# Another order of TensorE's work where one batch's MLP ends and the next one's begins

## The chip, the cores and the metric

The kernel runs on one core of a Trainium2 chip. The metric is device time in microseconds (us) of one execution. Three runs of the kernel before gave 1241.06, 1241.08 and 1241.23 us, so the median is 1241.08 us. All profile numbers come from one further, profiled execution that took 1240.99 us.

## What is computed

The reference is linear attention followed by a token mixer and a two-layer MLP, all in float32 accuracy, for 8 batches of 576 tokens and 512 features (8 heads of 64):

```python
def phi(x):
    proj = np.einsum('bhsd,df->bhsf', x, w_phi)
    proj = proj - np.max(np.abs(proj), axis=-1, keepdims=True)
    return np.concatenate([np.exp(proj), np.exp(-proj)], axis=-1)
q_p, k_p = (phi(q), phi(k))
kv = np.einsum('bhsf,bhsd->bhfd', k_p, v)
z = np.sum(k_p, axis=2)
num = np.einsum('bhsf,bhfd->bhsd', q_p, kv)
den = np.einsum('bhsf,bhf->bhs', q_p, z)[..., None] + 1e-06
x = num / den                       # heads side by side: (batch, 576, 512)
h = x.transpose(0, 2, 1) @ U @ V    # U: 576 x 32, V: 32 x 576
u = x + h.transpose(0, 2, 1)
out = u + np.maximum(u @ w_ch1, 0.0) @ w_ch2   # 512 -> 2048 -> 512
```

## The kernel before

**Two streams of work share TensorE.** The first is the attention of a batch: four pairs of heads, each cut into steps. `s_k0` projects k's 64 tail tokens (tile `pkt`) and the first head (`pk`), `s_k1` the second head, `s_q0` and `s_q1` project q (`pqt`, `pq`), `s_kv` makes k-features times v (`kv_ps`), `s_out` multiplies with the q-features (`xp`) and writes the result into `x` and, for the tail tokens, `xt`. `transpose_k` and `transpose_q` bring the raw k and q of the pair after the next one into shape (tiles `tT`, `T`). The second stream is the MLP of the batch before. Float32 accuracy is made of split values (`_hi`, `_lo`), so each product takes three matmuls.

**The MLP of a group of 512 tokens** (`Mixer`, line 564) begins with four `transposes(t)` (571): four TensorE transposes of `x[:, t, :]` into a PSUM tile `pt`, then ScalarE copies it to `uT_hi` and VectorE subtracts to get `uT_lo` (`split_t`, 223: lines 224 and 225). Then come 32 chunks from `chunks()` (635): `hidden(f)` (582, tile `ph`, twelve 512-column matmuls at line 588, then ScalarE's `h_hi` at 593 and VectorE's `h_lo` at 594) and `add(f)` (598, twelve matmuls at 605 into the four tiles `o`), in the order h0, h1, a0, h2, a1, ..., h15, a14, a15. Below, h15 stands for `hidden(15)`, a15 for `add(15)`, and h0', h1', a0' for those of the next group. `add(13)` also issues four loads of the token mixer's result from DRAM (`st`, line 612), and a15 ends in `finish()` (617): four VectorE additions of `o` to `st` (622) and the stores. There are nine groups: one for each batch, and one for the tail tokens of all batches, `x_tail`.

**The token mixer** (`Tokens`, 508) works on `x` in the last pair of a batch: `split`, `down`, then `up(0)` to `up(3)` and `up(NT)` for the tail tokens (549): one matmul (tile `vp`, 559), one VectorE addition into `x` or `xt` (560), one store.

**What limits the order.** PSUM has eight banks (line 67): three of tag `at` for all short-lived tiles (`pkt`, `pk`, `pq`, `xp`, `vp`, `T`, `pt`), one of tag `ph` for the hidden layer, and four of tag `o`. For groups 0 and 1, `pt` of tiles 2 and 3 uses `o` banks (line 572), and for the last two groups every second `ph` uses an `at` bank (583). `uT_hi` and `uT_lo` have one buffer each: no part of the new group's may be written before the old group's h15 has read the old one. `x` and `xt` have one buffer each too.

**Who sets the order.** In the first two batches a planner arranges all engines. From the third batch on, `ordered` (736) writes TensorE's order by hand (`manual_schedule`, line 860): `mix()` (655) takes the next chunk from the list `todo`. The other engines and the DMA queues are still ordered by the planner, from its own estimate of times, and then execute their queues in order. Within a batch `ordered` puts one chunk between any two attention steps. At a batch's end it runs `mix(len(todo) - HELD)` with HELD = 4, which leaves a13, h15, a14, a15, and then

```python
m.transposes(0)
tk.up(NT)
mix()               # a13
m.transposes(1)
m.transposes(2)
mix()               # h15
m.transposes(3)
do(far, "transpose_q")
todo.extend(m.chunks())
```

The next pair's turn then goes on with `s_k0`, a14, `s_out`, a15, `s_k1`, h0', `s_q0`, h1'. After the last batch, `x_tail` is loaded and its four transposes are laid between a13, h15, a14 and a15 (797 to 805).

Of the kernel before, what the change touches and what calls it, by code (L numbers as in the profile page):

```python
# [25 lines left out]
def tile_kernel(  # L26
# [13 lines left out]
    B, H, S, D = q.shape  # L40
# [7 lines left out]
    NT = S // P  # L48
# [41 lines left out]
    def load_w_phi():  # L90

        for g in range(2):
            nc.sync.dma_start(out=w_f[g * D:(g + 1) * D, :], in_=w_phi)
        nc.gpsimd.memset(w_two, 0.0)
        for g in range(2):
            r_ = slice(g * D, (g + 1) * D)
            nc.vector.tensor_copy(out=w_two[r_, g, :], in_=w_f[r_, :])
        nc.vector.tensor_copy(out=w_hi, in_=w_f)
        nc.vector.tensor_sub(w_lo, w_f, f32(w_hi))
# [62 lines left out]
    def load_uv():  # L162
        st = stage("u_st")[:, 0:(NT + 1) * R, :]
        sv = st.rearrange("p (t r) w -> p t r w", r=R)
        nc.sync.dma_start(
            out=sv[:, 0:NT], in_=U[0:SM].rearrange("(p t) r w -> p t r w", t=NT))
        for g in range(2):
            nc.sync.dma_start(out=sv[g * ST:(g + 1) * ST, NT], in_=U[SM:S])
        u_f = convert(st, "u").rearrange("p (t r) -> p t r", r=R)
        nc.vector.memset(f32(u_all[:, NT:NT + 2]), 0.0)  # L170
        parts = [(slice(0, P), slice(0, NT), slice(0, NT))]
        for g in range(2):
            parts.append((slice(g * ST, (g + 1) * ST), slice(NT + g, NT + g + 1), slice(NT, NT + 1)))
        for pr, to, of in parts:
            nc.vector.tensor_copy(out=u_all[pr, to, 0, :], in_=u_f[pr, of])
            nc.vector.tensor_sub(u_all[pr, to, 1, :], u_f[pr, of], f32(u_all[pr, to, 0, :]))
            for i in (2, 3):
                nc.vector.tensor_copy(out=u_all[pr, to, i, :], in_=f32(u_all[pr, to, 0, :]))

        for cs in (slice(0, SM // 2), slice(SM // 2, SM), slice(SM, S)):  # L180
            n = cs.stop - cs.start
            st = stage(f"v_st{cs.start}")[:, 0:n, :]
            for g in range(4):
                nc.sync.dma_start(out=st[g * R:(g + 1) * R], in_=V[:, cs])
            v_f = convert(st, f"v{cs.start}")
            vm = v_all[:, cs]
            if cs.stop <= SM:
                ps_ = slice(cs.start // NT, cs.stop // NT)
                v_f = v_f.rearrange("r (p t) -> r t p", t=NT)
                vm = v_all[:, 0:SM].rearrange("r (t p) -> r t p", t=NT)[:, :, ps_]  # L190
            nc.vector.tensor_copy(out=vm, in_=v_f)
            lo = slice(3 * R, 4 * R)
            nc.vector.tensor_sub(vm[lo], v_f[lo], f32(vm[lo]))
# [453 lines left out]
    def weights(upto):  # L647

        while done_f[0] < upto:
            f = next(blocks, None)  # L650
            done_f[0] = NFC if f is None else f - 1

    todo = []

    def mix(n=1):
        for _ in range(n):
            if todo:
                fn, f = todo.pop(0)
                if fn.__self__.g == 0 and done_f[0] < NFC:
                    weights(f + 2)  # L660
                fn(f)
# [22 lines left out]
    def keep_busy(n, here=False):  # L684
        wp = ps("busy", "ph")
        for _ in range(n):
            ins = nc.tensor.matmul(wp, zeros[:, 0:P], zeros, start=True, stop=True)
            if here:
                tc.keep_in_program_order(ins)

    HELD = 4
# [41 lines left out]

    ORDERED = 2

    def ordered(cur, nxt, x, xt, tk):

        for n, (b, j) in list(enumerate(pairs))[ORDERED * NPAIR:]:
            last = j == NPAIR - 1
            far = Pair(*pairs[n + 2]) if n + 2 < len(pairs) else None  # L740

            def do(who, name):
                if who is not None:
                    getattr(who, name)()

            if far is not None:
                far.load_v()
            do(nxt, "s_k0")
            mix()
            cur.s_out(x, xt)  # L750
            if j == 1:
                tk.split(0)
            if last:
                tk.split(1)
            mix()
            do(nxt, "s_k1")
            mix()
            do(nxt, "s_q0")
            mix()
            if last:  # L760
                tk.down(1)
            do(nxt, "s_kv")
            do(far, "transpose_k")
            mix()
            if last:
                tk.up(0)
                tk.up(1)
                mix()
                tk.up(2)
                tk.up(3)  # L770
            do(nxt, "s_q1")
            if j == 1:
                tk.down(0)
            if not last:
                mix()
                do(far, "transpose_q")
                mix()
            else:
                mix(len(todo) - HELD)
                m = Mixer(b, x)  # L780
                m.transposes(0)
                tk.up(NT)
                mix()
                m.transposes(1)
                m.transposes(2)
                mix()
                m.transposes(3)
                do(far, "transpose_q")
                todo.extend(m.chunks())
                if nxt is not None:  # L790
                    if b % 2 == 1:
                        xt = moe.tile([P, C], F32, tag="xt", name=f"xt{b + 1}")
                        nc.vector.memset(xt[ST:P], 0.0)
                    x = moe.tile([P, NT, C], F32, tag="x", name=f"x{b + 1}")
                    tk = Tokens(b + 1, x, xt)
            cur, nxt = nxt, far
        mix(len(todo) - HELD)
        x = moe.tile([P, NT, C], F32, tag="x", name="x_tail")
        nc.sync.dma_start(out=x, in_=u_dram[B])
        m = Mixer(B, x)  # L800
        for t in range(NT):
            m.transposes(t)
            mix()
        todo.extend(m.chunks())
        mix(len(todo))

    if True:
        cur = Pair(0, 0)
        load_w_phi()
        cur.load_v()  # L810
        keep_busy(6)
        cur.transposes()
        cur.s_k0()
        cur.s_k1_qt()
        cur.s_q0_only()
        nxt = Pair(0, 1)
        nxt.load_v()
        nxt.transposes()
        load_uv()
        cur.s_kv0_q1()  # L820
        cur.s_kv1()
        x = moe.tile([P, NT, C], F32, tag="x", name="x0")
        xt = moe.tile([P, C], F32, tag="xt", name="xt0")
        nc.vector.memset(xt[ST:P], 0.0)
        tk = Tokens(0, x, xt)
        for n, (b, j) in enumerate(pairs[:ORDERED * NPAIR]):

            far = Pair(*pairs[n + 2]) if n + 2 < len(pairs) else None
            if far is not None:
                far.load_v()  # L830
            if nxt is not None:
                step(nxt.s_k0)
            step(cur.s_out0, x, xt)
            if nxt is not None:
                step(nxt.s_k1_qt)
            step(cur.s_out1, x)
            if j == 1:
                tk.split(0)
            if j == NPAIR - 1:
                fill = []  # L840
                if nxt is not None:
                    fill = [nxt.s_q0_only, far.transposes, nxt.s_kv0_q1, nxt.s_kv1]
                tokens(tk, fill)
                if nxt is not None:
                    pace = Pace(32 - HELD, 34)
                    if b % 2 == 1:
                        xt = moe.tile([P, C], F32, tag="xt", name=f"xt{b + 1}")
                        nc.vector.memset(xt[ST:P], 0.0)
                    x = moe.tile([P, NT, C], F32, tag="x", name=f"x{b + 1}")
                    tk = Tokens(b + 1, x, xt)  # L850
            else:
                step(nxt.s_q0_only)
                if j == 1:
                    step(tk.down, 0)
                if far is not None:
                    step(far.transposes)
                step(nxt.s_kv0_q1)
                step(nxt.s_kv1)
            cur, nxt = nxt, far
        with tc.manual_schedule(engines={nc.tensor.engine}):  # L860
            ordered(cur, nxt, x, xt, tk)


# [29 lines left out]
```

## Time and profile before

| what | value |
|---|---|
| median of three runs | 1241.08 us |
| profiled execution: time, and span from the first to the last instruction | 1240.99 us, 1239.1 us |
| TensorE matmuls busy | 1177.0 us (95%) |
| TensorE weight loads busy | 957.5 us (77%) |
| VectorE, ScalarE, GpSimd busy | 679.5 us (55%), 545.7 us (44%), 205.4 us (17%) |
| granted TensorE clock, mean over the span | 0.985 |
| chain that ended last | TensorE 78%, VectorE 17%, ScalarE 2% |

The hand-ordered part begins near 250 us and ends at the span's end. In the views, a row of the timeline gives the start, the duration, the engine, the line, and in brackets the idle time of the engine ahead of it with the instruction that ended it. PE is TensorE, PEld its weight loads, DVE is VectorE, ACT is ScalarE, SPq the DMA-issuing queue of SyncE. Because matmuls are pipelined, their rows overlap: one 512-column matmul lasts 0.39 us in its row, and the next starts 0.23 us after it. The distance between starts is what counts.

### The profile page before, as it was taken

What the parts mean: (1) busy time and instruction counts of PE and PEld (TensorE: products, weight loads), DVE (VectorE), ACT (ScalarE), POOL (GpSimd) and SP (SyncE); (2) the same over time, 40 slices, a digit from 0 to 9 for tenths busy, and PEclk for the clock granted to TensorE, in tenths of its full rate; (3) what the DMA queues carried; (4) which work ended last, traced back from release to release, by engine and by line L of the source; (5) the groups of instructions that cost most, each with busy time, mean ns of one, the idle gap of its engine ahead of it and who ended that gap; (6) DMA issues with size and microseconds to landing.
All of it is one profiled execution on the core that took longest, in us unless ns stands there. A gap on an engine that the chain in (4) does not pass through costs nothing.

```text
span 1239.1 us, 22887 instructions
## 1 busy us (share of the span) xinstructions
PE 1177.0 (95%) x9266; PEld 957.5 (77%) x9280; DVE 679.5 (55%) x1469; ACT 545.7 (44%) x1230; POOL 205.4 (17%) x184
## 2 busy tenths in 40 slices
PE   8998888789999999999998999999999999999998
PEld 5666666568887888778887888778877887888886
DVE  6569989966464655456545646565545643212111
ACT  6667777745443445345434544354434531011110
POOL 3235444311110111011110111012101110000000
PEclk9999999999998999999999999899999999999999
DMA  4244344321131112221121113111222002100101
GB/s 132 53 143 126 101 142 138 113 99 43 30 92 41 42 30 61 71 63 30 56 68 54 40 30 96 41 38 30 61 70 64 27 1 83 66 1 1 34 1 34
DMA packets 95176, 75.70 MB, mean 61 GB/s; under 512 B 52320, under 2 KB 77280, under 8 KB 94944
## 3 DMA queue, kind: packets, MB, share of 16 engines
q1 hardware_dynamic: 95072, 74.25, 20.1%
q8 instruction: 73, 1.20, 0.4%
q14 instruction: 31, 0.25, 0.1%
HBM read 55.35 MB, written 18.87 MB: 60 GB/s over the span
## 4 chain that ended last, share of the span: by engine, by line
PE 78%; DVE 17%; ACT 2%; issue 1%; DMA 1%; SPq 0%; POOL 0%; DVEq 0%; POOLq 0%; ACTq 0%
PE o L605 28%; PE ph L588 28%; PE kv_ps L412 4%; PE xp L437 4%; DVE w L142 2%; PE pk L369 2%; PE T L298 2%; DVE w_ab L150 2%; PE pp L543 1%; PE kv_ps L403 1%; DVE uT_lo L225 1%; DVE h_lo L594 1%; DVE w_ab L147 1%; DVE w_lo L219 1%; DVE st L622 1%
## 5 line engine op out<-in xcount | busy, mean ns | idle before, releaser
L594 DVE SCALAR_TENSOR_TENSOR h_lo<-ph,h_hi 128x512 fp32r<-128x512 f32 x144 | 99.3, 689 | 285.9 <-ACT h_hi L593 285.6
L588 PE MATMUL ph<-uT_hi,w_hi 128*128 128x512 f32 x576 | 231.9, 403 | 10.0 <-DVE h_lo L594 8.2
L605 PE MATMUL o<-w_hi,h_hi 128*128 128x512 f32 x576 | 234.6, 407 | 5.0 <-ACT h_hi L593 5.0
L605 PE MATMUL o<-w_lo,h_hi 128*128 128x512 f32 x576 | 228.5, 397 | 0.0
L588 PE MATMUL ph<-uT_lo,w_hi 128*128 128x512 f32 x576 | 226.6, 393 | 1.3 <-DVE uT_lo L225 1.3
L588 PE MATMUL ph<-uT_hi,w_lo 128*128 128x512 f32 x576 | 227.1, 394 | 0.0
L605 PE MATMUL o<-w_hi,h_lo 128*128 128x512 f32 x576 | 225.4, 397 | 0.0
L593 ACT ACTIVATE h_hi<-ph 128x512 fp32r<-128x512 f32 x144 | 85.7, 595 | 275.8 <-PE ph L588 275.7
L333 POOL PARTITION_ALL_REDUCE qp<-qp x64 | 127.6, 1994 | 229.9 <-ACT qp L332 227.3
L588 PEld LDWEIGHTS ph<-uT_hi,w_hi 128*128 128x128 f32 x576 | 109.1, 189 | 35.2 <-DVE h_lo L594 11.7
L605 PEld LDWEIGHTS o<-w_hi,h_hi 128*128 128x128 f32 x576 | 110.5, 192 | 29.0 <-ACT h_hi L593 6.5
L605 PEld LDWEIGHTS o<-w_hi,h_lo 128*128 128x128 f32 x576 | 110.4, 192 | 25.1 <-issue 0.7
L588 PEld LDWEIGHTS ph<-uT_hi,w_lo 128*128 128x128 f32 x576 | 109.1, 189 | 24.0
L588 PEld LDWEIGHTS ph<-uT_lo,w_hi 128*128 128x128 f32 x576 | 109.5, 190 | 22.7 <-DVE uT_lo L225 1.6
L605 PEld LDWEIGHTS o<-w_lo,h_hi 128*128 128x128 f32 x576 | 110.5, 192 | 20.9
L333 POOL PARTITION_ALL_REDUCE qp_t<-qp_t x32 | 24.4, 763 | 472.0 <-ACT qp_t L332 472.0
L267 DVE TENSOR_TENSOR T<-T,T 64x512 fp32r<-64x512 f32 x96 | 66.2, 690 | 33.3 <-ACT T L266 32.2
L437 PE MATMUL xp<-kv,qp 128*64 128x65 f32 x2048 | 69.7, 222 | 4.8 <-DVE kp L373 2.3
L412 PEld LDWEIGHTS kv_ps<-vb,kp 128*64 128x64 f32 x2048 | 66.8, 137 | 8.7 <-issue 6.0
L266 ACT CAST T<-T 64x512 fp32r<-64x512 f32 x96 | 55.6, 579 | 38.2 <-DVE T L267 20.2
L437 PEld LDWEIGHTS xp<-kv,qp 128*64 128x64 f32 x2048 | 64.5, 138 | 9.8 <-issue 2.9
L412 PE MATMUL kv_ps<-vb,kp 128*64 128x65 f32 x2048 | 71.2, 223 | 0.6
(131 smaller groups left out, 1584.3 us busy)
## 6 DMA issues: line engine op xcount, KB each, us to landing
w<-in_moe_w_ch_dram SPq DMA_DIRECT2D x64, 256.0 KB, 2.7
raw<-in_k_dram SPq DMA_DIRECT2D x32, 256.0 KB, 3.0
raw<-in_q_dram SPq DMA_DIRECT2D x32, 256.0 KB, 2.6
vb<-in_v_dram SPq DMA_DIRECT2D x64, 128.0 KB, 2.7
u_dram<-x SPq DMA_DIRECT2D x32, 256.0 KB, 2.6
st<-u_dram SPq DMA_DIRECT2D x32, 256.0 KB, 3.8
out_dram<-st SPq DMA_DIRECT2D x32, 256.0 KB, 2.4
t_r<-in_k_dram SPq DMA_DIRECT2D x32, 32.0 KB, 2.6
```

What stands on the lines that cost most here:

```text
L142: nc.vector.tensor_scalar(out=halves[:, :, 0], in0=halves[:, :, 3], scalar1=0x7FF0, scalar2=None, op0=ALU.bitwise_and)
L150: nc.vector.scalar_tensor_tensor(out=a, in0=hi_w, scalar=-0x80000000, in1=a, op0=ALU.bitwise_and, op1=ALU.bitwise_or)
L266: nc.scalar.copy(out=dst[0:D], in_=src)
L267: nc.vector.tensor_sub(dst[D:2 * D], src, f32(dst[0:D]))
L298: nc.tensor.transpose(out=pT[:, c * P:(c + 1) * P], in_=self.raw[n][:, c // 2, c % 2, :], identity=ident)
L333: nc.gpsimd.partition_all_reduce(qp[:, 0, :], qp[:, 1, :], P, ReduceOp.absmax)
L412: nc.tensor.matmul(self.kv_v[z * HP:(z + 1) * HP, f, g, :], kp[:, t, f * F + z * HP:f * F + (z + 1) * HP], self.vb[:, g, t, :], start=Fals ...
L437: nc.tensor.matmul(xv[zs, c, :], qp[:, f, c * P + z * HP:c * P + (z + 1) * HP], self.kv[:, f, c // 2, :], start=(f == 0), stop=(f == 1), s ...
L588: nc.tensor.matmul(ph, l[:, c, fs], r[:, c, :], start=(n == 0), stop=(n == 3 * NCC - 1))
L593: nc.scalar.activation(out=h_hi, in_=ph, func=AF.Relu)
L594: nc.vector.scalar_tensor_tensor(out=h_lo, in0=ph, scalar=0.0, in1=f32(h_hi), op0=ALU.max, op1=ALU.subtract)
L605: nc.tensor.matmul(self.o[t], l[:, cs], r[:, f, :], start=(f == 0 and n == 0), stop=(f == NFC - 1 and n == 2))
```

## The change

A new function `boundary` sets the order at a batch's end. Three chunks are kept (h15, a14, a15) in place of four. Transposes 0 and 1 come together ahead of h15; `up(NT)` moves behind h15, followed by transposes 2, a14, transposes 3, `transpose_q`, a15, and h0' of the next group. So a14, a15 and h0' are no longer between `s_k0`, `s_out` and `s_k1` of the next pair; `s_out` follows `s_k0` without a chunk between them in the first pair of a batch (`if j > 0`), h1' stands between `s_out` and `s_k1`, and a0' behind `s_k1`. From there on, each place in a batch holds the chunk that is two further down the list, of the same kind as before. In the last pair of a batch one more `mix()` runs behind `s_q1`. At the entry into the hand-ordered part, three chunks (a14, a15 of batch 0, h0' of batch 1) run first. The tail group uses the same function without `up(NT)` and `transpose_q`; its load is issued before the last batch's remaining chunks, and a13 now precedes its transposes.

```diff
+    def boundary(m, *between):
+
+        between = list(between) + [[]] * 4
+
+        def run(k):
+            for fn, *args in between[k]:
+                fn(*args)
+
+        mix(len(todo) - 3)
+        m.transposes(0)
+        m.transposes(1)
+        mix()
+        run(0)
+        m.transposes(2)
+        run(1)
+        mix()
+        m.transposes(3)
+        run(2)
+        mix()
+        todo.extend(m.chunks())
+        mix()
+
     def ordered(cur, nxt, x, xt, tk):
...
             do(nxt, "s_k0")
-            mix()
+            if j > 0:
+                mix()
             cur.s_out(x, xt)
...
             do(nxt, "s_q1")
             if j == 1:
                 tk.down(0)
+            mix()
             if not last:
-                mix()
                 do(far, "transpose_q")
                 mix()
             else:
-                mix(len(todo) - HELD)
-                m = Mixer(b, x)
-                m.transposes(0)
-                tk.up(NT)
-                mix()
-                m.transposes(1)
-                m.transposes(2)
-                mix()
-                m.transposes(3)
-                do(far, "transpose_q")
-                todo.extend(m.chunks())
+                boundary(Mixer(b, x), [(tk.up, NT)], [], [(do, far, "transpose_q")])
...
-        mix(len(todo) - HELD)
         x = moe.tile([P, NT, C], F32, tag="x", name="x_tail")
         nc.sync.dma_start(out=x, in_=u_dram[B])
-        m = Mixer(B, x)
-        for t in range(NT):
-            m.transposes(t)
-            mix()
-        todo.extend(m.chunks())
+        boundary(Mixer(B, x))
         mix(len(todo))
...
         with tc.manual_schedule(engines={nc.tensor.engine}):
+            mix(3)
             ordered(cur, nxt, x, xt, tk)
```

## The prediction

> **What bounds the kernel now.** I read the page first.
>
> ```profile
> span 1239.1 us, 22887 instructions
> PE 1177.0 (95%) x9266; PEld 957.5 (77%) x9280; DVE 679.5 (55%) x1469; ACT 545.7 (44%) x1230; POOL 205.4 (17%) x184
> ```
>
> TensorE is the bound, and the change takes no matmul away. What can be won is the time in which TensorE stands still or runs slowly. So the second view is who TensorE waited for, in the window from 310 to 1060 us, which holds the six batch ends of batches 2 to 7:
>
> ```profile
> PE pt L575 <- DVE uT_lo L225: 8.4, 6, 1.4
> PE ph L588 <- DVE h_lo L594: 4.9, 5, 1.0
> PE pk L369 <- DVE kp_t L320: 3.7, 5, 0.8
> PE pk L369 <- DVE uT_lo L225: 3.5, 5, 0.7
> ```
>
> These four groups (total us, times, longest) are all that TensorE waits for in 750 us, and all are at batch ends. Third, the timeline of TensorE at one of them (batch 3), in its queue's order:
>
> ```profile
> 512.75 0.60 PE L575 MATMUL pt<-ident,x 128*128 128x128 f32 x4
> 513.11 0.48 PE L559 MATMUL vp<-pst,v_all 128*128 128x512 f32 x1
> 513.42 0.40 PE L605 MATMUL o<-w_hi,h_hi 128*128 128x512 f32 x1
> ...
> 516.19 1.03 PE L575 MATMUL pt<-ident,x 128*128 128x128 f32 x8
> 516.98 0.47 PE L588 MATMUL ph<-uT_hi,w_hi 128*128 128x512 f32 x1
> ...
> 519.60 0.39 PE L588 MATMUL ph<-uT_hi,w_lo 128*128 128x512 f32 x1
> 521.39 0.66 PE L575 MATMUL pt<-ident,x 128*128 128x128 f32 x4 [1.40 <-DVE uT_lo L225]
> ...
> 522.68 0.30 PE L343 MATMUL pkt<-w_hl,tail_T 128*128 128x128 f32 x1
> ...
> 523.78 0.50 PE L369 MATMUL pk<-w_hl,T 128*128 128x256 f32 x2 [0.70 <-DVE uT_lo L225]
> 525.11 0.58 PE L369 MATMUL pk<-w_hl,T 128*128 128x256 f32 x2 [0.83 <-DVE kp_t L320]
> ...
> 534.96 0.63 PE L369 MATMUL pk<-w_hl,T 128*128 128x256 f32 x4
> ...
> 539.99 0.50 PE L588 MATMUL ph<-uT_hi,w_hi 128*128 128x512 f32 x1 [0.97 <-DVE h_lo L594]
> ```
>
> Three `pt` tiles fill the three `at` banks, and none can be emptied before h15 has read the old `uT`. When h15 ends (last matmul at 519.60), the fourth `pt` has to wait until ScalarE and VectorE have evicted the first. Then `T`, `pkt` and two `pk` need banks too, with nothing long between them. 0.97 is the wait of h1' for the one `ph` bank, which h0' left 0.9 us before.
>
> The idle time is only half of the loss. Fourth, the windows view, columns: stretch, its length, PE, PEld, DVE, ACT and POOL busy, granted clock. The first two rows are batch 3's stretch from transposes 1 to `s_k1`, and the sum over the same stretch of batches 2 to 6:
>
> ```profile
> 516.19:534.96 18.77, 15.83 (x132) 12.53 (x131) 11.06 (x25) 6.33 (x13) 0.00 (x0) 0.91 0.06 17
> ...
> sum 95.51, PE 81.24 PEld 63.87 DVE 53.94 ACT 31.65 POOL 0.00; mean PE 16.25 PEld 12.77 DVE 10.79 ACT 6.33 POOL 0.00
> ...
> 521.90:525.30 3.40, 1.86 (x11) 1.24 (x10) 3.33 (x8) 2.30 (x6) 0.00 (x0) 1.00 0.28 77
> 525.30:528.70 3.40, 3.40 (x10) 2.72 (x10) 2.50 (x4) 1.35 (x4) 0.00 (x0) 0.50 0.00 0
> ...
> 1051.00:1054.40 3.40, 3.37 (x17) 2.87 (x18) 2.37 (x4) 1.31 (x3) 0.00 (x0) 1.00 0.41 130
> ```
>
> Behind the 3.4 us that were busy for only 1.86, the granted clock is 0.50 for 3.4 us. After batch 7, whose end has the 1.40 wait alone (no further pair follows), it stays at 1.00.
>
> **The loss now, by the stretch.** What would it take without waits? Undisturbed steps from the same batch:
>
> ```profile
> 477.84 0.22 PE L343 MATMUL pkt<-w_hl,tail_T 128*128 128x128 f32 x1
> ...
> 478.80 0.39 PE L588 MATMUL ph<-uT_hi,w_hi 128*128 128x512 f32 x1
> ...
> 486.75 0.64 PE L369 MATMUL pk<-w_hl,T 128*128 128x256 f32 x4
> ```
>
> From 477.84 to 486.75 run `s_k0` (0.96), a chunk, `s_out` and a chunk: 8.91. Two transposed tiles take 0.79 (516.19 to 516.98), h15 takes 2.85 (516.98 to 519.60 plus the 0.23 between matmuls), one more `pt` 0.36 (512.75 to 513.11), `T` as much. Sum 13.3, five times 66.5. Against 95.51 that is a loss of 29.0 us. Of it 8.4 x 5/6 + 3.5 + 3.7 = 14.2 is recorded as idle; the other 14.8 is the half clock and the restart of the pipeline. The 4.9 of h1' lies outside the stretch. So batches 2 to 6 lose 33.9 us, 6.8 each.
>
> **The change, part by part.** The chunks stay 32 for each group, so the moves of chunks cost nothing by themselves. What the moves remove: between the four `pt`, `T` and `s_k0` there now stand h15, a14, a15 and h0', 2.85 us each, so `T` and `s_k0` find their banks evicted; and h1' comes after `s_k0` and `s_out`, over 3 us behind h0'. All 33.9 go.
>
> What is late next? First `pt` 2, which now needs a bank right after h15 and `up(NT)`: two banks hold `pt` 0 and 1, the third `vp`.
>
> ```profile
> 520.03 1.56 ACT L224 CAST uT_hi<-pt 128x512 fp32r<-128x512 f32 x3 [6.48 <-PE ph L588]
> 520.64 1.89 DVE L225 TENSOR_TENSOR uT_lo<-pt,uT_hi 128x512 fp32r<-128x512 f32 x3 [3.32 <-ACT uT_hi L224]
> 513.62 0.69 DVE L560 TENSOR_TENSOR xt<-xt,vp 64x512 f32<-64x512 f32 x1 [4.19 <-PE vp L559]
> ```
>
> VectorE's addition from `vp` starts 0.51 after `vp` (513.11 to 513.62) and takes 0.69; TensorE follows some 0.06 later, so `pt` 2 starts 1.26 after `vp` where 0.31 is its free distance (513.11 to 513.42): 0.95 lost. Should it get `pt` 0's bank, it starts 1.56 after (519.83 to 521.39), 1.25 lost; with VectorE's addition ahead of that, 1.25 + 0.69 - 0.3 = 1.64. I take 0.95, because the addition is ready before `uT_lo` is. Five times 4.75, and at batch 7's end 0.95 stands in place of 1.40: -0.45. Moving `up(NT)` behind h15 delays its store by some 3 us; what is behind it on the SP queue, the load of q that waits for `transpose_q` and the final stores, is due later.
>
> Second, `s_out` right behind `s_k0`: its first `xp` needs the bank of `pkt`, which VectorE's `kp_t` releases.
>
> ```profile
> 478.70 0.29 DVE L320 TENSOR_TENSOR kp_t<-pkt,mk_t 128x128 f32<-128x128 f32 x1
> 524.67 0.29 DVE L320 TENSOR_TENSOR kp_t<-pkt,mk_t 128x128 f32<-128x128 f32 x1
> ```
>
> In the undisturbed step `kp_t` ends at 478.99, 0.19 after `s_k0`'s own end, 0.25 with the signal. At the batch end now, with VectorE crowded, it ends at 524.96, 2.28 after `pkt` began, which is 1.3 to 1.4 too late. After the change the four additions of a15 run during h0', and only h0's `h_lo` competes. Nearer to the first: 0.6, five times 3.0.
>
> Third, h0' directly behind a15 needs the last `uT_lo`. Here a15 and `T` are the cover. Batch 7 shows that queue:
>
> ```profile
> 1051.03 0.66 PE L575 MATMUL pt<-ident,x 128*128 128x128 f32 x4 [1.40 <-DVE uT_lo L225]
> ...
> 1052.68 0.68 DVE L225 TENSOR_TENSOR uT_lo<-pt,uT_hi 128x512 fp32r<-128x512 f32 x1
> 1055.16 2.73 DVE L622 TENSOR_TENSOR st<-st,o 128x512 f32<-128x512 f32 x4 [1.79 <-PE o L605]
> ```
>
> There `uT_lo` ends 2.3 after its `pt` began, and h0' is due 0.36 + 0.36 + 2.85 = 3.6 after: covered by 1.2 us, as long as the additions (2.73) stand behind it in VectorE's queue, as here. The additions themselves wait for the four `st` loads that a13 issues; all loads of that tile, from issue to landing:
>
> ```profile
> DMA to landing us min/median/max: 2.1/2.9/4.7
> ```
>
> They have over 8 us (two `pt`, h15, a14 and the rest). Cost of the third 0.
>
> Fourth, the clearing of `xt` on VectorE, which waits for the store of `up(NT)`, twice (behind batches 3 and 5):
>
> ```profile
> 516.84 0.48 DVE L793 MEMSET xt<- 64x512 f32 x1 [1.81 <-DMA u_dram<-xt]
> ```
>
> It starts 2.5 after the addition's end (514.31). Placed ahead of `uT_lo` it would cost up to 3 us each time, 6 in all; behind it nothing. I take 0.
>
> Fifth, the entry into the hand-written order. Waits of TensorE in the first 310 us, and one row of the timeline:
>
> ```profile
> PE pk L369 <- DVE uT_lo L225: 1.6, 1, 1.6
> PE ph L588 <- DVE uT_lo L225: 1.3, 1, 1.3
> 271.35 0.50 PE L588 MATMUL ph<-uT_hi,w_hi 128*128 128x512 f32 x1 [0.73 <-DVE h_lo L594]
> ```
>
> These 3.6 go. But `pt` 2 and 3 of batch 1 lie in `o` banks (line 572), free only after a15's additions, and h0' now comes at once: it waits for an eviction of 1.79 (519.60 to 521.39), or 2.4 with a second tile, and `s_out` pays its 0.6. Net -1.0; between -4 (nothing waits) and +3 (the additions, 2.7, stand first). The tail group has the same four chunks around its transposes as before, without `up`: 0.
>
> Sum against the profiled execution: 1240.99 - 29.0 - 4.9 + 4.75 - 0.45 + 3.0 - 1.0 = 1213.4, and as it stands 0.09 below the median, **1213 us**.
>
> A rule to weigh against the clock rows: the Trainium skill, "TensorE: Matmul & The Clock Gate", section "HAM oscillation — how this bites in real kernels", lets the clock fall only for idle gaps above some 3.4 us. The trace disagrees: no gap here exceeds 1.40, and the clock falls to 0.50. By the page's rule the half clock would have another cause and stay.
>
> **The rivals.**
> - *Half clock stays.* Something other than these gaps, or the new gaps, still halves the clock at the batch ends: the 14.8 aren't won, 1228 us. For it: 1.86 busy of 3.4 sufficed. Against: batch 7's end, with 1.40 idle, kept 1.00, and the new gaps are 0.95 and 0.6, two chunks and more apart. The rule just named belongs here.
> - *Both new waits at their upper ends* (1.64 and 1.4), with one half-clock window of 3.4 at each (1.7 lost): 1213 + 5 x (0.69 + 0.8 + 1.7) + 3 for the entry = 1232.
> - *Slower: h0' becomes the stall.* The planner puts the last `uT_lo` behind the four additions and both subtractions for `T` in VectorE's queue. Then h0' idles about 0.5 + 0.64 + 3 x 0.69 + 0.1 = 3.3 us behind a15, and the clock halves for two windows (3.4 lost); with 1.64 and 1.4 that is 9.7 a batch end. Above 6.8 the change loses: 1241 + 5 x 2.9 + 3 = 1258. Against it: the two rows of batch 7 above.
> - *It doesn't do what it says:* the order of the other engines is the planner's, and it moves evictions so that the same waits return under other names. 1241.
>
> **How the numbers follow.** Forecast 0.68, half clock stays 0.11, upper ends 0.09, no change 0.04, slower 0.08. Faster is 0.88. The measurement can tell about 0.2% (2.5 us) from no change. The range runs from 1206 (`pt` 2 without a wait, -4.75, and the entry at -4) to 1234, which takes in the first two rivals and the 6 of `xt`; it leaves out the other two, 0.12, and some 0.05 below.
>
> **What would show it.** Right: the four groups of waits give way to `pt` <- DVE of about 0.8 us, six times, and `xp` <- DVE `kp_t` of some 0.4, no `ph` <- `h_lo` at batch ends, no 0.50 clock at batches 2 to 6, busy time unchanged apart from the clock. Wrong: `ph` <- `uT_lo` behind a15, or 0.50 at the batch ends.

## The result and the profile after

The changed kernel takes 1210.96 us (median of four runs, 1209.04 to 1212.18) against 1241.07 us; the ratio is 0.9758, interval 0.9741 to 0.9775. The profiled execution took 1212.18 us, 28.8 less than that of before, against a forecast of 27.6 less.

Of the page after, first the span and the busy times:

```profile
span 1210.4 us, 22881 instructions
PE 1159.1 (96%) x9266; PEld 948.5 (78%) x9280; DVE 670.6 (55%) x1469; ACT 544.6 (45%) x1230; POOL 205.4 (17%) x184
```

TensorE's matmuls are as many as before (x9266), and yet it is busy for 17.9 us less. One reason is the half clock: in the half-clock window of the kernel before that begins at 525.30, 512-column matmuls start 0.43 us apart (525.49 and 525.92), in place of 0.23. So more has gone than waits. Second, who TensorE waited for from 250 to 1060 us, entry included (total us, times, longest):

```profile
PE pt L575 <- DVE xt L560: 4.7, 6, 0.8
PE o L605 <- DVE h_lo L594: 2.0, 1, 2.0
PE xp L430 <- DVE kp_t L320: 1.7, 6, 0.3
PE o L605 <- ACT h_hi L593: 1.7, 1, 1.7
PE ph L588 <- ACT uT_hi L224: 0.7, 1, 0.7
PE ph L588 <- DVE uT_lo L225: 0.2, 1, 0.2
```

The four groups of before are gone. Two new ones come instead: `pt` waits at six batch ends, `xp` at five and once at the entry. The four that come once belong to the entry. The same batch end as was shown before (batch 3), timeline of TensorE, chunks cut to their first matmul:

```profile
510.35 1.03 PE L575 MATMUL pt<-ident,x 128*128 128x128 f32 x8
511.14 0.48 PE L588 MATMUL ph<-uT_hi,w_hi 128*128 128x512 f32 x1
...
513.96 0.40 PE L559 MATMUL vp<-pst,v_all 128*128 128x512 f32 x1
515.14 0.66 PE L575 MATMUL pt<-ident,x 128*128 128x128 f32 x4 [0.79 <-DVE xt L560]
515.55 0.48 PE L605 MATMUL o<-w_hi,h_hi 128*128 128x512 f32 x1
...
518.41 0.60 PE L575 MATMUL pt<-ident,x 128*128 128x128 f32 x4
518.84 0.60 PE L298 MATMUL T<-ident,raw 128*128 128x128 f32 x4
...
522.05 0.39 PE L588 MATMUL ph<-uT_hi,w_hi 128*128 128x512 f32 x1
...
524.77 0.22 PE L343 MATMUL pkt<-w_hl,tail_T 128*128 128x128 f32 x1
...
525.90 0.45 PE L430 MATMUL xp<-kv,qp_t 128*64 128x65 f32 x8 [0.29 <-DVE kp_t L320]
...
528.15 0.50 PE L588 MATMUL ph<-uT_hi,w_hi 128*128 128x512 f32 x1
...
531.01 0.63 PE L369 MATMUL pk<-w_hl,T 128*128 128x256 f32 x4
```

h0' at 522.05 follows a15 without a wait, and so does h1' at 528.15 after `s_out`. And the stretch from these first transposes to `s_k1` in the windows view (length, busy times, granted clock, then the DMA engines' share and GB/s):

```profile
510.35:531.01 20.66, 19.59 (x161) 16.44 (x160) 13.10 (x28) 7.42 (x16) 0.00 (x0) 1.00 0.21 71
```

The clock is 1.00 where it was 0.91, and it is 1.00 over the whole stretch from 300 to 1200 us. The stretch holds more than its counterpart of before, so it is set against its own clean length: two tiles 0.79, h15 2.85, `vp` 0.31, `pt` 0.36, a14 2.85, `pt` and `T` 0.72, a15 2.85, h0' 2.72, `s_k0` 0.96, `s_out` 2.25, h1' 2.86, together 19.5. The loss is 1.1 us a batch end where it was 6.8. Five times 5.7 is 28.5 of the 28.8 us. A second count agrees: an undisturbed `s_k0` that comes once in each batch returns every 134.3 us before (343.08 to 880.41, four batches) and every 128.3 us after (349.88 to 863.20), which is 6.0 less for one batch end.

### The profile page after: what moved, and what is told of

Read it like the earlier page. It is cut to its first block, busy times and chain, and to the rows that moved or that the text cites. A ratio compares the mean times of both kernels' runs of the same rounds, so it can differ in the third digit from the quotient of the medians.

```text
span 1210.4 us, 22881 instructions
## 1 busy us (share of the span) xinstructions
PE 1159.1 (96%) x9266; PEld 948.5 (78%) x9280; DVE 670.6 (55%) x1469; ACT 544.6 (45%) x1230; POOL 205.4 (17%) x184
## 3 DMA queue, kind: packets, MB, share of 16 engines
q1 hardware_dynamic: 95072, 74.25, 20.5%
## 4 chain that ended last, share of the span: by engine, by line
PE 82%; DVE 13%; DMA 2%; ACT 1%; issue 1%; SPq 1%; POOL 0%; DVEq 0%; POOLq 0%; ACTq 0%
PE o L605 30%; PE ph L588 29%; PE xp L437 4%; PE kv_ps L412 4%; DVE w L142 2%; PE T L298 2%; PE pk L369 2%; DMA w<-in_moe_w_ch_dram 2%; DVE w_ab L150 2%; PE pp L543 1%; PE kv_ps L403 1%; PE pt L575 1%; DVE w_ab L147 1%; DVE w_lo L219 1%; PE pq L392 1%; PE xp L430 1%
## 5 line engine op out<-in xcount | busy, mean ns | idle before, releaser
L605 PE MATMUL o<-w_lo,h_hi 128*128 128x512 f32 x576 | 225.5, 392 | 0.0
```

The lines of the kernel that those rows point to most:

```text
L605: nc.tensor.matmul(self.o[t], l[:, cs], r[:, f, :], start=(f == 0 and n == 0), stop=(f == NFC - 1 and n == 2))
```

## The experiments

The theory is that of the prediction, "chunks between": a14, a15 and h0' now stand where evictions were waited for, and with the waits goes the half clock that they cause. One rival is that the new order of the four transposes around h15 does it; another, that the half clock has a cause of its own. All runs are compared with the kernel before on the same chip (1240.1 to 1241.1 us).

**e1_order_only.** The kernel before with the transposes' new order alone:

```diff
-                mix(len(todo) - HELD)
+                mix(len(todo) - 3)
                 m = Mixer(b, x)
                 m.transposes(0)
-                tk.up(NT)
-                mix()
                 m.transposes(1)
-                m.transposes(2)
                 mix()
+                tk.up(NT)
+                m.transposes(2)
                 m.transposes(3)
```

> The kernel before with the new order of transposes alone: pt 0 and pt 1 together ahead of h15, up(NT) behind it, then pt 2, pt 3 and transpose_q; a14, a15 and h0' stay between the next pair's steps. Theory 'chunks between' (the gain comes from a14, a15 and h0' standing where evictions would be waited for, and from the half clock that these waits cause): pt 2 waits 0.8 us for a bank, then pt 3, T, pkt and pk wait one after another, 3 us or more at a batch end, the clock still falls to 0.50 there, h1' still waits 0.97: 1238 to 1246 us, no gain. Rival 'transposes around h15' (the gain comes from two pt instead of three being held over h15): the waits are gone but for 0.8 a batch end, near 1218 us.

Measured: 1238.1 us against 1240.37, ratio 0.9975 (0.9962 to 0.9988). TensorE's waits from 300 to 1060 us:

```profile
PE ph L588 <- DVE h_lo L594: 4.9, 5, 1.0
PE pk L369 <- DVE kp_t L320: 4.8, 5, 1.0
PE pt L575 <- DVE xt L560: 4.7, 6, 0.8
PE pkt L343 <- DVE uT_lo L225: 2.6, 5, 0.5
PE pk L369 <- DVE uT_lo L225: 2.4, 5, 1.0
```

They sum to 19.4 us, against 20.5 before: the wait at `pt` got shorter, and `pkt` and `pk` took what it gave. The clock falls to 0.50 at three of the five batch ends, before at all five. Order alone is worth some 2 us (1.5 to 4.7 by the interval), where the expectation had none; the time is at the lower end of its range.

**e2_chunks_only.** The changed kernel with the old order of transposes inside `boundary`:

```diff
-        mix(len(todo) - 3)
+        mix(len(todo) - 4)
         m.transposes(0)
-        m.transposes(1)
-        mix()
         run(0)
+        mix()
+        m.transposes(1)
         m.transposes(2)
-        run(1)
         mix()
         m.transposes(3)
         run(2)
-        mix()
+        mix(2)
```

> The changed kernel with the old order of transposes (pt 0, up(NT), a13, pt 1, pt 2, h15, pt 3, transpose_q) and a14, a15, h0' behind it ahead of s_k0. Theory 'chunks between': only pt 3's wait of 1.40 us comes back, in place of 0.78, six times, and T may wait 0.3: 1214 to 1218 us, clock 1.00 at the batch ends of batches 2 to 6, since one gap of 1.4 alone did not lower it at batch 7. Rival 'transposes around h15': most of the gain is lost, 1230 us or more.

Measured: 1215.22 us, ratio 0.9797 (0.9781 to 0.9814). Its waits from 300 to 1060 us, and the 3.4 us with the wait in batch 3's end and those behind them:

```profile
PE pt L575 <- DVE uT_lo L225: 8.4, 6, 1.4
PE xp L430 <- DVE kp_t L320: 1.4, 5, 0.3
```

```profile
511.70:515.10 3.40, 2.00 (x13) 1.36 (x12) 2.39 (x4) 2.98 (x6) 0.00 (x0) 1.00 0.00 0
515.10:518.50 3.40, 3.40 (x17) 2.81 (x16) 2.38 (x5) 0.83 (x2) 0.00 (x0) 1.00 0.26 77
```

The 1.40 waits are all back, and still 25 of the 30 us are won: the chunks carry the gain, and the order of the transposes adds some 4. Not all of the 4 lies at the batch ends: a seventh wait of 1.4 us comes at the tail group. One gap of 1.40 leaves the clock at 1.00, at all of these batch ends.

**e4_zero_fill.** The kernel before with work for TensorE in its gaps, and no wait shortened (`zfill_o` holds the four `o` tiles at the ends of batches 2 to 6, and is empty elsewhere):

```diff
...
+    def zfill(n):
+        for i in range(2 * n if zfill_o else 0):
+            nc.tensor.matmul(
+                zfill_o[i % 4][:, 0:2 * P], zero_bf, ident.bitcast(BF16), start=False, stop=False)
...
                 pk = self.ps(f"pk{g}{s}_").rearrange("p (t n f) -> p t n f", t=2, n=2)
+                zfill(3 + s)
...
+                zfill(6)
                 m.transposes(3)
```

> The kernel before, with matmuls of zeros (128x256, bf16, added to the four o tiles, so that nothing changes in the result) put in TensorE's queue ahead of pt 3 (12), of the first pk (6) and of the second pk (8) at the ends of batches 2 to 6: the same waits are there, but TensorE works through them. Theory 'the waits cause the half clock': no 0.50 at these batch ends, and of the 14.8 us of half clock and restart most is won although no wait is shortened: 1226 to 1233 us. Rival 'half clock of another cause', as a rule of gaps over 3.4 us would have it: 0.50 stays, 1240 us or more.

Measured: 1231.77 us, ratio 0.9927 (0.9907 to 0.9946), 8.6 us less. Batch 3's end in its timeline, and the windows view of the stretch that had the half clock:

```profile
517.42 1.48 PE L699 MATMUL o<-ident,zero_bf 128*128 128x256 bf16 x12
518.98 0.65 PE L576 MATMUL pt<-ident,x 128*128 128x128 f32 x4
519.62 0.63 PE L298 MATMUL T<-ident,raw 128*128 128x128 f32 x4
...
520.52 0.83 PE L699 MATMUL o<-ident,zero_bf 128*128 128x256 bf16 x6
521.37 0.50 PE L370 MATMUL pk<-w_hl,T 128*128 128x256 f32 x2
521.72 1.05 PE L699 MATMUL o<-ident,zero_bf 128*128 128x256 bf16 x8
```

```profile
519.00:533.50 14.50, 14.46 (x137) 11.71 (x138) 12.27 (x28) 5.49 (x13) 0.00 (x0) 1.00 0.26 92
```

The three waits are as long as before: in both kernels `pt` 3 starts 1.56 us behind the end of h15's matmuls, the first `pk` 1.10 behind `pkt`, the second 1.33 behind the first. Filling them with 3.4 us of useless work made the kernel faster. The clock stays at 1.00, here and over the whole stretch from 300 to 1220 us, so it was the standing still of TensorE that halved it, and the rival of another cause falls. Of the 14.8 us of half clock and restart 8.6 came back. An estimate of the half clock's share: the windows view of the kernel before has seven windows of 3.4 us at 0.50 at these five batch ends (two each at batches 2 and 5), which lose at most half of 23.9 us, 11.9. Part of the rest may be waiting that no row records as idle: `T` starts 0.64 us behind `pt` 3 here (0.43 in the changed kernel, 518.41 to 518.84), about as long as VectorE takes for each `uT_lo` that frees a bank (three in 1.89 us before). That `T` waits for these is argued from the times, not tested.

**e3_up_first.** Can the remaining wait of `pt` 2 be had too? The changed kernel with `run(0)`, that is `up(NT)`, ahead of the first transposes:

```diff
         mix(len(todo) - 3)
+        run(0)
         m.transposes(0)
         m.transposes(1)
         mix()
-        run(0)
         m.transposes(2)
```

> The changed kernel with up(NT) ahead of transposes 0 in place of behind h15, so that vp's bank is free when h15 ends. If the remaining 0.78 us wait of pt 2 is for the bank of vp or of pt 0 with all three banks held over h15, it goes, six times 0.87 with the restart: 1205 to 1207 us against 1211, and no group pt <- DVE at the batch ends. If pt 2 instead waits for something else (x, uT), the time stays at 1211.

Measured: 1204.70 us, ratio 0.9709 (0.9693 to 0.9726); the wait for `vp`'s bank is gone, as all of TensorE's waits from 300 to 1060 us show:

```profile
PE xp L430 <- DVE kp_t L320: 1.4, 5, 0.3
```

The time is a little below the expected 1205 to 1207. In the traces one batch takes 127.4 us (348.88 to 858.37, four batches) against 128.3, 0.96 less, where the expectation had 0.87. The difference of the two medians, 6.3 us, is partly the scatter of the runs.

**e5_pool_clears_xt.** The entry. In the trace of the changed kernel, VectorE behind h15 of batch 0's MLP:

```profile
254.09 1.29 DVE L225 TENSOR_TENSOR uT_lo<-pt,uT_hi 128x512 fp32r<-128x512 f32 x2
256.57 0.48 DVE L856 MEMSET xt<- 64x512 f32 x1 [1.19 <-DMA u_dram<-xt]
257.08 0.69 DVE L594 SCALAR_TENSOR_TENSOR h_lo<-ph,h_hi 128x512 fp32r<-128x512 f32 x1
```

The clearing of `xt` waits for a store to land, and `h_lo` of h15, which a15 needs at once, stands behind it in the queue. The clock halves in the window that follows:

```profile
257.10:260.50 3.40, 2.68 (x6) 2.15 (x7) 1.92 (x3) 0.00 (x0) 0.00 (x0) 0.50 0.08 33
```

So e3 with `nc.gpsimd.memset` for the three `nc.vector.memset(xt[ST:P], 0.0)`, the same order on TensorE:

> Run e3 (up(NT) first) with the clearing of xt on GpSimd in place of VectorE, TensorE's order the same. At the entry of e3's trace a15 of batch 0 waits 2.0 us for h15's h_lo, which stands in VectorE's queue behind the clearing, and that behind the landing of up(NT)'s store. If the clearing is what holds h_lo, its start moves from 257.2 to about 255.5 us, TensorE's wait shrinks from 3.66 to about 2.0, and the half clock behind it may go: 1 to 4 us less than e3, 1201 to 1204 us. If the store is hidden anyway, the wait stays at 3.66 and the time at 1204.7.

Measured: 1202.66 us, ratio 0.9696 (0.9683 to 0.971). TensorE's waits there (from 250 to 300 us) and the following window:

```profile
PE o L605 <- ACT h_hi L593: 1.7, 1, 1.7
...
PE o L605 <- DVE h_lo L594: 0.2, 1, 0.2
```

```profile
255.30:258.70 3.40, 2.97 (x12) 2.16 (x13) 2.80 (x5) 0.18 (x1) 0.52 (x1) 1.00 0.14 39
```

The 2.0 for `h_lo`, which e3 has as well, became 0.2, and the clock stays at 1.00. The time is 2 us below e3, but the two intervals overlap; the mechanism is shown, its price only about.

**e6_old_entry.** e3 without the three chunks ahead of `ordered`, and with the old first pair:

```diff
-            if j > 0:
+            if j > 0 or n == ORDERED * NPAIR:
                 mix()
...
-            mix(3)
             ordered(cur, nxt, x, xt, tk)
```

> Run e3 with the entry into the hand-written order as in the kernel before: no three chunks ahead, a14 after s_k0, a15 after s_out, h0' after s_k1 in the first pair; all later batch ends as in e3. If the new entry costs (3.66 us of waiting for h15's h_lo, 1.1 for uT, and a half clock, against 1.6, 1.5 and 0.7 before), it comes out 1 to 4 us below e3. If the entry is neutral, as the prediction's term of -1.0 has it within its bounds, 1204 to 1206 us.

Measured: 1204.2 us, ratio 0.9705 (0.9692 to 0.9719), level with e3 within the scatter of the runs. The new entry is neutral as far as this shows: it trades waits of 1.6, 1.5 and 0.9 for e3's 3.7 (2.0 and 1.7) and 1.0.

**e7_h0_after_k0 and e8_all.** The last regular wait, `xp` for `kp_t`. In e7, e3 with h0' moved from ahead of `s_k0` to behind it; e8 has e5's clearing as well:

```diff
         m.transposes(3)
         run(2)
         mix()
         todo.extend(m.chunks())
-        mix()
...
-            if j > 0:
-                mix()
+            mix()
             cur.s_out(x, xt)
...
-            mix(3)
+            mix(2)
```

> Run e3 with h0' moved from ahead of s_k0 to between s_k0 and s_out. The last regular wait, xp <- kp_t of 0.28 us, should go, six times 0.3 to 0.4: 1202 to 1204 us. Rival: h0' behind s_k0 delays s_k0's features on ScalarE and VectorE and h1' comes only 2.3 us behind h0', so that the ph bank is waited for instead: no gain, or up to 1 us worse.

> up(NT) first, the clearing of xt on GpSimd, and h0' between s_k0 and s_out together. If the three effects are independent they add: 1199 to 1203 us, no regular wait of TensorE left at the batch ends; against the changed kernel's 1211 about 0.8% less.

Measured: e7 1217.88 us, ratio 0.9814 (0.98 to 0.9827); e8 1215.11, 0.9796 (0.9781 to 0.981). Both expectations missed: e7 is 13 us worse than e3, e8 12 us worse than e5. In e7, the second `pk` and VectorE's queue ahead of it:

```profile
525.42 0.47 PE L369 MATMUL pk<-w_hl,T 128*128 128x256 f32 x2 [1.98 <-DVE T L267]
```

```profile
521.75 0.68 DVE L267 TENSOR_TENSOR T<-T,T 64x512 fp32r<-64x512 f32 x1
522.47 1.88 DVE L622 TENSOR_TENSOR st<-st,o 128x512 f32<-128x512 f32 x3
524.27 0.28 DVE L318 TENSOR_REDUCE mk_t<-pkt 128x1 f32<-128x128 f32 x1
524.58 0.69 DVE L267 TENSOR_TENSOR T<-T,T 64x512 fp32r<-64x512 f32 x1
```

`T`'s second subtraction stands behind three of a15's additions, and the bank of `T` is wanted by the second `pk`. With h0' ahead of `s_k0`, 2.7 us of matmuls cover this. So h0' had a cover to give that neither the prediction nor the expectation had seen.

**e9_q_early and e10_q_early_h0_late.** To test that reading, `transpose_q` goes ahead of a13, in e5 (e9) and in e8 (e10):

```diff
+        run(2)
         mix(len(todo) - 3)
         run(0)
...
         m.transposes(3)
-        run(2)
```

> Run e5 with transpose_q moved from behind pt 3 to ahead of a13, so that T is evicted before VectorE gets the four additions of a15. h0' stays ahead of s_k0. If T's eviction is already hidden under h0', nothing changes: 1202 to 1204 us, the xp wait of 0.28 stays.

> Run e8 (h0' between s_k0 and s_out) with the same early transpose_q. In e7 and e8 pk waited 2.0 us for T's last subtraction, which stood behind the four additions in VectorE's queue. If that queue is the cause, the wait goes and the time falls from 1215 to 1200 to 1204 us, level with e9 or up to 2 us below. If s_k0 directly behind a15 waits for VectorE anyway (for kp_t and the additions themselves), 1207 us or more, and pk or pkt still wait over 0.5 us.

Measured: e9 1202.58 us, ratio 0.9698 (0.9685 to 0.9712); e10 1203.37, 0.9704 (0.9691 to 0.9717), 12 us below e8. TensorE waits for nothing in e10 between 300 us and the end. With `T` out of VectorE's queue the place of h0' no longer matters; the queue was the cause. The 0.3 of `xp` is not worth a measurable time. e5 and e9 are the fastest versions, 3% below the kernel before.

## Why the prediction was right, point by point

- *The loss now* of 6.8 us a batch end, 33.9 in all, goes: right, by the four lost groups of waits. What stays, 1.1 a batch end, was forecast as 1.55.
- *`pt` 2 waits for `vp`'s bank, 0.95:* right. It starts 1.18 after `vp` (513.96 to 515.14) where 1.26 was worked out, 0.87 lost, six times, and e3 removed it by giving that bank back earlier.
- *`xp` behind `kp_t`, 0.6:* right in its mechanism, too large: 0.29 idle. The value from the undisturbed step, 0.25, would have been nearly exact, because VectorE is free again when `s_k0` comes. Five times 0.31 is 1.6 us forecast too much, more than the whole error of the sum, 1.2.
- *h0' behind a15, 0:* right, no wait at a batch end. But the reason given for h0's place was half of it: its place also hides `T`'s eviction (e7, e10).
- *The half clock* goes with the waits: right, and shown by e4, so the rival falls. The 14.8 us may also have held waiting for banks that no row records as idle (argued at e4). The rule of the Trainium skill ("TensorE: Matmul & The Clock Gate", section "HAM oscillation — how this bites in real kernels"), gaps above some 3.4 us, does not agree with these runs: none of the gaps at these batch ends was over 1.40 us, and filling them brought the clock back.
- *The clearing of `xt`, 0 behind batches 3 and 5:* right there. At the entry, where it was not looked for, it cost 2.0 us of waiting.
- *The entry, -1.0:* about 0 (e6). The step that failed is its account of what is late next: it has h0' waiting 1.8 to 2.4 for `uT`, which was 0.9; in its place a15 waits 3.7 for h15's own evictions, since a14 had been run before h15 by the planner, and the clock halves behind it.

The mechanism was right, but that the sum came within 1.2 us is partly luck: the 1.6 too much at `xp` and the 1.0 gained at the entry that did not come had opposite signs.

## What to carry to other kernels

Count a wait of TensorE by the stretch it lies in, against the same steps undisturbed, not by its idle time: here 14.2 us of waits at batch ends cost 29.0. Long matmul chunks belong behind the steps whose evictions the next steps need, and it pays to ask of each chunk which evictions it hides; h0' hid one worth 13 us that the waits view of e3, where it is hidden, does not list. A slow or waiting instruction in an in-order queue, such as a clearing that waits for a store, harms whoever stands behind it: at the entry TensorE waited 2.0 us behind it, and 0.2 once it was gone from that queue (e5).

## What the runs showed of the hardware

The half clock depends on where a wait falls, not on its length alone. It comes on a grid: in the kernel before it begins at 388.8, 525.3, 658.4, 791.6 and 928.1 us, 40, 39, 39 and 40 times 3.41 us apart. In e7 the same wait of 2.0 us occurs at five batch ends. Here at the first and the second of them (windows view: length, PE, PEld, DVE, ACT and POOL busy, clock):

```profile
391.60:395.00 3.40, 1.41 (x10) 1.16 (x9) 3.32 (x7) 0.96 (x2) 0.00 (x0) 1.00 0.77 292
395.00:398.40 3.40, 3.40 (x10) 2.62 (x9) 1.88 (x4) 1.52 (x4) 0.00 (x0) 0.50 0.07 24
521.30:524.70 3.40, 2.14 (x12) 1.64 (x10) 3.31 (x7) 0.96 (x2) 0.00 (x0) 1.00 0.67 233
524.70:528.10 3.40, 2.68 (x13) 2.32 (x14) 2.66 (x6) 0.78 (x3) 0.00 (x0) 1.00 0.39 151
```

The first wait lies wholly within one window of the clock's grid, TensorE is busy for 1.41 of it, and the next window runs at 0.50. The second is split over two windows with 2.14 and 2.68 busy, and the clock stays; so it does at the other three. Busy time alone does not separate the cases: 1.93 busy at e7's fifth batch end (910.41 to 913.83) and 2.00 in e2 left the clock at 1.00, but 2.19 at batch 4 in the kernel before did not:

```profile
655.00:658.40 3.40, 2.19 (x12) 1.44 (x12) 3.37 (x7) 2.33 (x6) 0.00 (x0) 1.00 0.20 44
658.40:661.90 3.50, 2.88 (x8) 2.43 (x9) 3.07 (x7) 1.67 (x5) 0.00 (x0) 0.51 0.09 32
```

What exactly is counted stays open.
